# Keys and values loaded and sorted per batch item in a Sinkhorn attention kernel with a maxout layer behind it

## The chip, the cores and the metric

The kernel runs on one NeuronCore of a Trainium2 chip. The metric is the device time of one execution in microseconds (us), where lower is better. The trace also gives a "span", from the first to the last recorded event; in the profiled runs quoted here it is 1.7 to 2.2 us shorter than the time. TensorE runs the matmuls, VectorE ("DVE" in the profile), ScalarE ("ACT") and GpSimd ("POOL") the rest; "SP" only issues transfers. A transfer issued by SP or ACT is an HWDGE transfer, one issued by GpSimd an SWDGE transfer.

## The reference, cut to what matters

```python
# q, k, v: 4 batch items x 8 heads x 768 tokens x 64, fp32; sort_net: 4 x 8 x 8 x 8
P = sort_net
for _ in range(5):                       # Sinkhorn
    P = exp(P - rowmax(P)); P = P / rowsum(P); P = P / colsum(P)
k_sorted = einsum('bhij,bhjcd->bhicd', P, k_blocks)   # 8 blocks of 96 tokens
v_sorted = einsum('bhij,bhjcd->bhicd', P, v_blocks)
attn = softmax(q_block @ k_sorted_block.T / 8)        # block i with block i only
x = (attn @ v_sorted_block).transpose(0, 2, 1, 3).reshape(3072, 512)
out = maximum(x @ w1, x @ w2) @ w_out                 # 512 -> 1024 -> 512
```

The kernel rewrites the last line as relu(x @ (w1 - w2)) @ w_out + x @ (w2 @ w_out), so that one half of the hidden products is computed once for the weights instead of per token.

Of the kernel before, what the change touches and what calls it, by code (L numbers as in the profile page):

```python
# [15 lines left out]
def kernel(  # L16
# [16 lines left out]

# [16 lines left out]
    NSB = 2  # L50
# [5 lines left out]
    big = ctx.enter_context(tc.tile_pool(name="big", bufs=1))  # L56
    qpool = ctx.enter_context(tc.tile_pool(name="qpool", bufs=2))
# [13 lines left out]
    fill = const.tile([128, 512], FP32, tag="fill", name="fill")  # L71
# [33 lines left out]

    def load_q(b):
        t = qpool.tile([128, H, R * D], BF16, tag="q_raw", name="q_raw")
        nc.gpsimd.dma_start(out=t, in_=q[b].rearrange("h (p r) d -> p h (r d)", r=R))
        q_raw[b] = t

    k_raw = big.tile([128, BLK * D], BF16, tag="k_raw", name="k_raw")
    v_raw = big.tile([128, BLK * D], BF16, tag="v_raw", name="v_raw")
    k_src = k.rearrange("b (a par) (j c) d -> par (b a) j (c d)", par=2, j=NB)
    v_src = v.rearrange("b (a par) (j c) d -> par (b a) j (c d)", par=2, j=NB)

    def load_k(sb, chunks):
        n = BLK * D // 3
        for ci in chunks:
            for par in range(2):
                nc.gpsimd.dma_start(  # L120
                    out=k_raw[par * 64 : par * 64 + 64, ci * n : (ci + 1) * n],
                    in_=k_src[par, sb * 8 : sb * 8 + 8, :, ci * n : (ci + 1) * n],
                )

    VCH = 3

    def load_v(sb, chunks):
        n = BLK * D // VCH
        for ci in chunks:
            for par in range(2):  # L130
                nc.gpsimd.dma_start(
                    out=v_raw[par * 64 : par * 64 + 64, ci * n : (ci + 1) * n],
                    in_=v_src[par, sb * 8 : sb * 8 + 8, :, ci * n : (ci + 1) * n],
                )
# [13 lines left out]
    def load_w_columns(dst, src, t):  # L148
# [6 lines left out]
    load_v(0, range(VCH))  # L155
    ident = const.tile([128, 128], BF16, tag="ident", name="ident")
    make_identity(nc, ident)

    mask16 = const.tile([128, 16], BF16, tag="mask16", name="mask16")
    nc.gpsimd.memset(mask16, 1.0)  # L160
    nc.gpsimd.affine_select(
        out=mask16, in_=mask16, compare_op=ALU.is_ge, fill=0.0, base=0,
        pattern=[[-NB, 16]], channel_multiplier=1,
    )
    nc.gpsimd.affine_select(
        out=mask16, in_=mask16, compare_op=ALU.is_ge, fill=0.0, base=NB - 1,
        pattern=[[NB, 16]], channel_multiplier=-1,
    )
    load_q(0)
    load_k(0, range(3))  # L170


    v_dc = big.tile([128, D * BLK + 32], BF16, tag="v_dc", name="v_dc")

    def turn_v(eng, c0, c1):
        dst = v_dc[:, 0 : D * BLK].rearrange("p (d c) -> p d c", c=BLK)[:, :, c0:c1]
        src = v_raw.rearrange("p (c d) -> p d c", d=D)[:, :, c0:c1]
        if eng == "A":
            nc.scalar.copy(out=dst, in_=src)
        else:  # L180
            nc.vector.tensor_copy(out=dst, in_=src)

    for t in range(4):
        load_w_columns(w2_sb, moe_w2, t)
        load_w_columns(w1_sb, moe_w1, t)
    load_w(wo_sb, moe_w_out)
    load_q(1)


# [3 lines left out]
    maskJ = const.tile([128, NB], FP32, tag="maskJ", name="maskJ")  # L193
    sels = []
# [17 lines left out]
    def selections():  # L212

        nc.vector.reduce_sum(
            out=maskJ, in_=ident.rearrange("p (m j) -> p j m", j=NB), axis=AX.X
        )
        for sb in range(NSB):
            sel = const.tile([G, 2, 8, NB], BF16, tag=f"sel{sb}", name=f"sel{sb}")
            src = ident[0:G, sb * 16 : sb * 16 + 16].rearrange("p (gp par) -> p par gp", par=2)
            for par in range(2):  # L220
                nc.vector.tensor_copy(
                    out=sel[:, par], in_=src[:, par, :].to_broadcast([G, 8, NB])
                )
            sels.append(sel)
# [3 lines left out]
    def block_diagonals(sb, n=0):  # L228

        pe = ps_f32("pe")  # L230
        keep_streaming(pe, n)
        nc.tensor.matmul(
            pe[:, 0 : NB * NB],
            sels[sb].rearrange("p a g j -> p (a g j)"),
            p_bf.rearrange("p i j -> p (i j)"),
            start=True,
            stop=True,
        )
        pm = const.tile([128, NB, NB], FP32, tag=f"pm{sb}", name=f"pm{sb}")
        nc.vector.tensor_tensor(  # L240
            out=pm,
            in0=pe[:, 0 : NB * NB].rearrange("p (i j) -> p i j", j=NB),
            in1=maskJ.to_broadcast([128, NB, NB]).transpose([0, 2, 1]),
            op=ALU.mult,
        )
        pt = const.tile([128, NB], FP32, tag=f"pt{sb}", name=f"pt{sb}")
        nc.vector.reduce_sum(out=pt, in_=pm, axis=AX.X)
        bv = const.tile([128, 16, NB], BF16, tag=f"bv{sb}", name=f"bv{sb}")
        nc.vector.tensor_tensor(
            out=bv,  # L250
            in0=mask16.to_broadcast([128, 16, NB]),
            in1=pt.to_broadcast([128, NB, 16]).transpose([0, 2, 1]),
            op=ALU.mult,
        )
        bk = const.tile([128, 8, NB], BF16, tag=f"bk{sb}", name=f"bk{sb}")
        nc.vector.tensor_tensor(out=bk, in0=bv[:, 0:8, :], in1=bv[:, 8:16, :], op=ALU.add)
        bd_v[sb] = bv.rearrange("p m i -> p (m i)")
        bd_k[sb] = bk.rearrange("p m i -> p (m i)")



    kT = big.tile([128, 64 * BLK + 32], BF16, tag="kT", name="kT")
    nc.vector.memset(kT[:, 64 * BLK :], 0.0)
    nc.vector.memset(v_dc[:, D * BLK :], 0.0)
    e_bufs = []
    for n in range(NE):
        t = big.tile([BLK, 8 * BLK + 32], BF16, tag=f"e{n}", name=f"e{n}")
        nc.vector.memset(t[:, 8 * BLK :], 0.0)
        e_bufs.append(t)
    v_sb = big.tile([BLK, 128, D + 2], BF16, tag="v_sb", name="v_sb")  # L270
    nc.vector.memset(v_sb[:, :, D : D + 1], 1.0)
    xT = big.tile([128, B, 2, HP, TCH], BF16, tag="xT", name="xT")

    def q_transposes(b, half):
# [3 lines left out]
        qv = q_raw[b].rearrange("p h (r d) -> p h r d", r=R)  # L278
        ps = ps_bf16("tq_ps")
        for n in range(2 * R):  # L280
            hp, r = half * 2 + n // R, n % R
            for h2 in range(2):
                nc.tensor.matmul(  # L283
                    ps[h2 * 64 : h2 * 64 + 64, n * 128 : (n + 1) * 128],
                    qv[:, 2 * hp + h2, r, :],
                    ident,
                    is_transpose=True,
                    start=True,
                    stop=True,
                )  # L290
# [7 lines left out]
    def sort_k(sb, t, n=0):  # L298
        kv = k_raw.rearrange("p (c d) -> p c d", d=D)
# [3 lines left out]
        for c in range(16):  # L303
            for par in range(2):
# [5 lines left out]
                    bd_k[sb][r0 : r0 + 64, :],  # L310
# [4 lines left out]
            kT[:, 0 : 64 * BLK].rearrange("p (m c) -> p m c", c=BLK)[:, :, t * 16 : (t + 1) * 16],  # L315
            ps.rearrange("p (c m) -> p m c", m=64),
            1024,
        )

    def sort_v(sb, t, n=0):  # L320
        ps = ps_f32("v_ps")
        keep_streaming(ps, n)
        for d in range(8):
            nc.tensor.matmul(  # L324
                ps[:, d * 128 : (d + 1) * 128],
                v_dc[:, (t * 8 + d) * BLK : (t * 8 + d) * BLK + 128],
                bd_v[sb],
                start=True,
                stop=True,
            )  # L330
        evac(
            v_sb[:, :, t * 8 : (t + 1) * 8],
            ps[0:BLK].rearrange("p (d m) -> p m d", m=128),
            1024,
        )
# [3 lines left out]
    def scores(b, u, n=0):  # L339
        ih, hp = divmod(u, HP)  # L340
        gp = (b % 2) * 4 + hp
        ps = ps_f32("s_ps")
        keep_streaming(ps, n)
        for ii in range(4):
            i = ih * 4 + ii
            for h2 in range(2):
                nc.tensor.matmul(  # L347
                    ps[:, h2 * 512 + ii * BLK : h2 * 512 + (ii + 1) * BLK],
                    kT[h2 * 64 : h2 * 64 + 64, (gp * 8 + i) * BLK : (gp * 8 + i) * BLK + 128],
                    qT[b][h2 * 64 : h2 * 64 + 64, hp, :, i * PB : (i + 1) * PB],  # L350
# [13 lines left out]
    def values(b, u, n=0):  # L364
        ih, hp = divmod(u, HP)
        gp = (b % 2) * 4 + hp
        e = e_tiles.pop((b, u))
        ps = ps_f32("o_ps")
        keep_streaming(ps, n)
        for h2 in range(2):  # L370
            for ii in range(4):
# [3 lines left out]
                    v_sb[:, h2 * 64 + gp * 8 + ih * 4 + ii, 0:65],  # L375
# [8 lines left out]
        x = xpool.tile([BLK, 4, 2, D], BF16, tag="x", name="x")  # L384
        nc.vector.tensor_tensor(  # L385
            out=x.rearrange("p i t d -> p t i d"),
            in0=ov[:, :, :, 0:D],
            in1=rs.to_broadcast([BLK, 2, 4, D]),
            op=ALU.mult,
        )  # L390
        load["D"] += 900
        x_tiles[b, u] = x

    def x_transposes(b, t, eng=None):

        ih, hh = divmod(t, 2)
        ps = ps_bf16("tx_ps")
        for n in range(2):
            x = x_tiles.pop((b, t * 2 + n))
            for ii in range(4):  # L400
                m = n * 4 + ii
                nc.tensor.matmul(  # L402
# [249 lines left out]
```

## The kernel before: the parts that the change touches

GpSimd loads everything, casting fp32 to bf16. Keys and values come for two batch items at once. The 64 rows (head group x block) of even heads go to partitions 0 to 63, those of odd heads to 64 to 127.

```python
k_src = k.rearrange("b (a par) (j c) d -> par (b a) j (c d)", par=2, j=NB)
def load_k(sb, chunks):                  # load_v is the same
    n = BLK * D // 3
    for ci in chunks:
        for par in range(2):
            nc.gpsimd.dma_start(
                out=k_raw[par * 64 : par * 64 + 64, ci * n : (ci + 1) * n],
                in_=k_src[par, sb * 8 : sb * 8 + 8, :, ci * n : (ci + 1) * n])
# order of issue: v of items 0 and 1, identity, q of item 0, k of items 0 and 1,
# w2 and w1 by columns, w_out, q of item 1; the rest of q, k, v later
```

The matmuls that sort need "block diagonals" made of P. For v, the tokens are first "turned" (d and c swapped by a strided copy). The program's order fixes what each engine does next:

```python
for it in range(4):
    sinkhorn(it)
    if it == 1: selections()
turn_v("A", 0, 8); sinkhorn(4); turn_v("A", 8, 24); turn_v("D", 24, 32)
block_diagonals(0, 8 * 512)              # 8 x 512 columns of fill ahead of it
... # four more turns, on ACT ("A") and VectorE ("D")
for t in range(8):
    sort_v(0, t, 4 * 512 if t == 0 else 0)
    if t in (3, 5): q_transposes(0, (t - 3) // 2)
for t in range(6):
    sort_k(0, t, {2: 384, 4: 512}.get(t, 0))
... # scores, values and transposes of item 0, then the loop over items:
    # MoE products ("units") of item b, between which stand "steps" of item b + 1
```

`keep_streaming(ps, n)` multiplies a tile of zeros, n columns long, only to keep TensorE busy ("fill"). All matmul results go through four PSUM buffers in turn; to "evict" one is to copy its result to SBUF, by ACT or VectorE. `p_bf` is the finished P in bf16. "MoE" is the code's name for the maxout layer; its "h products" are the hidden ones, and its "weight product" is w2 @ w_out. The "granted clock" is the share of its full clock that TensorE is allowed.

The softmax here doesn't subtract the row's maximum and nothing guards it: scores larger than these inputs give would overflow.

## Time and profile before

| | before |
|---|---|
| time, median of 3 runs | 191.15 us (190.85 to 194.3) |
| span of the profiled run | 189.5 us |
| first MoE product starts | 37.11 us |
| start of the last eviction that waits for TensorE | 185.06 us |
| TensorE, VectorE, ACT busy | 94%, 48%, 46% |

Until 37 us the kernel waits for loads and fills TensorE with zeros; after it TensorE does useful work nearly without a gap.

### The profile page before, as it was taken

The page shows a single profiled execution, that of the slowest core. Times are in us where ns is not written, and L with a number is a line of the kernel's source. Part 1 is how long each engine was busy: PE and PEld are TensorE (multiplying, and loading weights), DVE is VectorE, ACT ScalarE, POOL GpSimd, SP SyncE. Part 2 cuts the span into 40 slices and gives each one's busy share as a digit, 9 for nine tenths or more (in the row PEclk, how much of TensorE's full clock was granted, in tenths as well). Part 3 has the DMA queues.
Part 4 walks back from the last instruction along what each step waited for, and adds up shares of the span by engine and source line. Part 5 has one row for each costly group of instructions (what it writes and reads, how often), then busy time and mean ns, then how long its engine had stood idle before and what let it go on. Part 6 is the DMA issues. An engine that isn't in the chain of part 4 may idle for free.

```text
span 189.5 us, 4458 instructions
## 1 busy us (share of the span) xinstructions
PE 177.5 (94%) x1992; PEld 105.5 (56%) x1992; DVE 90.5 (48%) x172; ACT 88.0 (46%) x103; POOL 25.8 (14%) x47
## 2 busy tenths in 40 slices
PE   6989996799999999999999999999999999999990
PEld 3436755667645455467776445467655456654440
DVE  4887944853431552991476155445553133430030
ACT  3286846877345323059977414237634132631100
POOL 7732465312430000000000000000000000000000
PEclk9999999999999999999999999999999999999998
DMA  2999999999999922230000030230000322000241
GB/s 38 171 200 213 207 197 194 204 205 214 210 209 201 193 58 84 111 112 3 3 3 0 0 114 0 111 114 0 3 0 3 111 111 93 22 0 0 111 156 69
DMA packets 16243, 19.17 MB, mean 101 GB/s; under 512 B 2400, under 2 KB 11616, under 8 KB 16224
## 3 DMA queue, kind: packets, MB, share of 16 engines
q0 software_dynamic: 12896, 12.59, 40.1%
q1 hardware_dynamic: 3328, 6.30, 8.9%
q8 instruction: 15, 0.25, 0.5%
q14 instruction: 4, 0.03, 0.1%
HBM read 25.17 MB, written 6.29 MB: 166 GB/s over the span
## 4 chain that ended last, share of the span: by engine, by line
PE 75%; DMA 11%; DVE 5%; ACT 4%; issue 2%; POOL 1%; ACTq 0%; POOLq 0%
PE out_ps L503 23%; PE h_ps L475 22%; PE out_ps L511 11%; DMA k_raw<-in_k_dram 7%; PE wc_ps L448 4%; DMA v_raw<-in_v_dram 4%; PE o_ps L372 3%; PE s_ps L347 3%; PE tx_ps L402 2%; PE k_ps L307 2%; PE v_ps L324 2%; PE tq_ps L283 2%; DVE o L98 1%; ACT qT L96 1%; PE tw_ps L427 1%
## 5 line engine op out<-in xcount | busy, mean ns | idle before, releaser
L503 PE MATMUL out_ps<-wo_sb,g 128*128 128x512 bf16 x192 | 45.4, 379 | 1.6 <-DVE o L98 0.9
L475 PE MATMUL h_ps<-xT,w_sb 128*128 128x384 bf16 x256 | 45.8, 326 | 0.5 <-ACT xT L96 0.4
L355 ACT ACTIVATE e<-s_ps 96x768 bf16<-96x768 f32 x32 | 24.7, 806 | 23.7 <-PE s_ps L347 23.7
L475 PEld LDWEIGHTS <-w_sb 128*128 128x128 bf16 x256 | 23.7, 98 | 15.1 <-issue 0.4
L503 PEld LDWEIGHTS <-g 128*128 128x128 bf16 x192 | 17.9, 97 | 21.0 <-issue 1.7
L511 PE MATMUL out_ps<-wc,xT 128*128 128x512 bf16 x96 | 24.6, 379 | 0.0
L385 DVE TENSOR_TENSOR x<-o_ps,rs 96x512 bf16<-96x512 f32 x32 | 22.0, 686 | 1.1
L485 ACT ACTIVATE g<-h_ps 128x768 bf16<-128x768 f32 x19 | 15.5, 814 | 15.0 <-PE h_ps L475 14.2
L487 DVE TENSOR_SCALAR g<-h_ps 128x768 bf16<-128x768 f32 x13 | 12.5, 958 | 19.6 <-PE h_ps L475 19.6
L96 ACT COPY o<-out_ps 128x1024 f32<-128x1024 f32 x7 | 7.1, 1013 | 26.8 <-PE out_ps L511 22.3
L383 DVE RECIPROCAL rs<-o_ps 96x8 f32<-96x8 f32 x32 | 6.4, 200 | 23.3 <-PE o_ps L372 23.3
L511 PEld LDWEIGHTS <-xT 128*128 128x128 bf16 x96 | 9.4, 98 | 11.3
L372 PEld LDWEIGHTS <-e 96*128 96x128 bf16 x256 | 11.7, 98 | 3.4
L372 PE MATMUL o_ps<-v_sb,e 96*128 96x65 bf16 x256 | 13.5, 194 | 0.1
L98 DVE COPY o<-out_ps 128x1024 f32<-128x1024 f32 x4 | 4.9, 1225 | 17.2 <-PE out_ps L511 17.2
L96 ACT CAST v_sb<-v_ps 96x1024 bf16<-96x1024 f32 x11 | 10.7, 1022 | 4.0 <-PE v_ps L324 4.0
L347 PE MATMUL s_ps<-qT,kT 64*128 64x96 bf16 x256 | 10.0, 205 | 1.6 <-issue 1.2
L78 PE MATMUL pe<-fill 128*128 128x512 f32 x16 | 9.9, 785 | 1.5 <-DVE fill L72 1.5
L98 DVE COPY xT<-tx_ps 128x768 bf16<-128x768 bf16 x7 | 6.7, 955 | 7.7 <-PE tx_ps L402 7.7
L347 PEld LDWEIGHTS <-kT 64*128 64x128 bf16 x256 | 6.2, 94 | 7.1 <-issue 4.6
L98 DVE CAST kT<-k_ps 128x1024 bf16<-128x1024 f32 x5 | 6.1, 1225 | 8.0 <-PE k_ps L307 7.9
L96 ACT COPY xT<-tx_ps 128x768 bf16<-128x768 bf16 x9 | 7.2, 795 | 4.2 <-PE tx_ps L402 4.2
(70 smaller groups left out, 174.5 us busy)
## 6 DMA issues: line engine op xcount, KB each, us to landing
out_dram<-o SPq DMA_DIRECT2D x11, 512.0 KB, 2.8
v_raw<-in_v_dram POOLq DMA_DIRECT2D x12, 256.0 KB, 11.6
q_raw<-in_q_dram POOLq DMA_DIRECT2D x4, 768.0 KB, 13.9
k_raw<-in_k_dram POOLq DMA_DIRECT2D x12, 256.0 KB, 12.0
w_sb<-in_moe_w_dram POOLq DMA_DIRECT2D x8, 256.0 KB, 10.6
wo_sb<-in_moe_w_out_dram POOLq DMA_DIRECT2D x2, 512.0 KB, 12.4
out_dram<-o SPq DMA_DIRECT2D x2, 256.0 KB, 2.0
p_sb<-in_sort_net_dram SPq DMA_DIRECT2D x1, 8.0 KB, 1.7
```

Of the source, the lines that this page charges most:

```text
L78: nc.tensor.matmul(ps[:, 0:w], fill[:, 0:128], fill[:, 0:w], start=True, stop=True)
L96: nc.scalar.copy(out=out_ap, in_=in_ap)
L98: nc.vector.tensor_copy(out=out_ap, in_=in_ap)
L347: nc.tensor.matmul(ps[:, h2 * 512 + ii * BLK : h2 * 512 + (ii + 1) * BLK], kT[h2 * 64 : h2 * 64 + 64, (gp * 8 + i) * BLK : (gp * 8 + i) * ...
L355: nc.scalar.activation(out=e[:, 0 : 8 * BLK].rearrange("p (t f) -> p t f", t=2), in_=ps[0:BLK].rearrange("p (t f) -> p t f", t=2)[:, :, 0 ...
L372: nc.tensor.matmul(ps[:, h2 * 512 + ii * 65 : h2 * 512 + (ii + 1) * 65], e[:, (h2 * 4 + ii) * BLK : (h2 * 4 + ii) * BLK + 128], v_sb[:, h2 ...
L385: nc.vector.tensor_tensor(out=x.rearrange("p i t d -> p t i d"), in0=ov[:, :, :, 0:D], in1=rs.to_broadcast([BLK, 2, 4, D]), op=ALU.mult,)
L475: nc.tensor.matmul(ps[:, m * 512 : m * 512 + TCH], w1_sb[:, hp, fb * 128 : (fb + 1) * 128], xT[:, b, ch, hp, :], start=(hp == 0), stop=(hp ...
L485: nc.scalar.activation(out=g, in_=src, func=AF.Relu)
L487: nc.vector.tensor_scalar(out=g, in0=src, scalar1=0.0, scalar2=None, op0=ALU.max)
L503: nc.tensor.matmul(dst, g_tiles[b, ch, fb // 2][:, fb % 2, off : off + 128], wo_sb[:, fb, :], start=(fb == 0), stop=False,)
L511: nc.tensor.matmul(dst, xT[:, b, ch, hp, off : off + 128], wc[:, hp, :], start=False, stop=(hp == HP - 1),)
```

## The change

The intent: load and sort only what batch item 0 needs before the first MoE product, and put the sorting of item 1 between the products. Keys lie as 128 rows (head, block, half of the block's tokens). SP loads the first pieces of v and half of q of item 0 as fp32 (HWDGE) beside GpSimd's loads. Output units are cut in halves so that steps stand more evenly between them. The tile of zeros for the fill becomes bf16 instead of fp32: the first fill was 16 matmuls of 512 columns in 9.85 us, and is now 24. Cut to its core:

```diff
+    for m in range(HB // VF):                       # 3 pieces of 16 tokens
+        t = opool.tile([128, 2, 512], FP32, tag="o", name="v_f32")
+        nc.sync.dma_start(out=t[0:64, :], in_=v_src[0, :, m * VF * D : (m + 1) * VF * D])
+    for n in range(2):
+        nc.sync.dma_start(
+            out=q_f32[:, n * 4 : n * 4 + 4, :], in_=q_half[0, :, n * 4 : n * 4 + 4, :])
-    load_v(0, range(VCH))
+    load_v(0, HB)                                   # only tokens 48 to 96 of each block
+    make_identity(nc, ident32)                      # fp32
-    load_q(0)
-    load_k(0, range(3))
+    load_k(0)                                       # item 0 only
+    load_w_columns(w2_sb, moe_w2, 0)
+    load_w_columns(w1_sb, moe_w1, 0)
+    nc.gpsimd.dma_start(out=q_bf, in_=q_half[1])    # other half of q, bf16
     ... # other weights
+    load_v(1)
+    load_k(1)
     load_q(1)
 ...
+    def q_first(t, n=0):                            # fp32 products with the identity
+        keep_streaming(ps, n)
+        ...
+                nc.tensor.matmul(ps[...], q_f32[:, hp + 4 * h2, r * D : (r + 1) * D],
+                                 ident32, start=True, stop=True)
 ...
+        if it == 0:
+            masks(0)
+            q_out.append(q_first(0, 12288))         # 24 x 512 columns of bf16 fill
+        if it == 1:
+            q_out.append(q_first(1))
+            turn_v(first, "A", 0, 8, v_f32[0])      # ACT, between the Sinkhorn exps
 ...
+        4: [lambda: block_diagonals(1), lambda: turn(second, 0)],
+        5: [lambda: turn(second, 24), lambda: selections(2)],
+        6: [lambda: turn(second, 48), lambda: pair_q(1, 0), lambda: pair_q(1, 1)],
+        7: [lambda: turn(second, 72), lambda: block_diagonals(2), lambda: selections(3)],
+        8: [lambda: block_diagonals(3), lambda: load_v(2), lambda: load_v(3)],
 ...
+    def moe_out_last(ti, pieces):                   # last two tiles, in pieces
+                o = opool.tile([128, w], FP32, tag=f"o{n0}{m}", name="o", bufs=1)
```

## The prediction

> **What bounds the kernel now.** I read the engine totals first, then the slices, then the chain of waits in order of time, and last the timeline of single engines in the first 40 us.
>
> ```profile
> PE 177.5 (94%) x1992; PEld 105.5 (56%) x1992; DVE 90.5 (48%) x172; ACT 88.0 (46%) x103; POOL 25.8 (14%) x47
> PE   6989996799999999999999999999999999999990
> DMA  2999999999999922230000030230000322000241
> ```
>
> TensorE looks full from end to end, but its first eight slices (4.74 us each) hold many matmuls of the zero tile "fill", which only keep it running. The transfers are dense just there. The chain says what those slices wait for:
>
> ```profile
> 1.32 1.29 POOL v_raw L131 x2
> 2.62 7.11 DMA v_raw<-in_v_dram
> 9.73 0.28 issue
> 10.01 13.94 DMA k_raw<-in_k_dram
> 23.95 0.04 issue
> 24.00 1.27 PE k_ps L307 x63
> ...
> 36.26 0.81 ACT xT L96
> 37.07 0.04 issue
> 37.11 1.46 PE h_ps L475 x8
> ```
>
> Two transfers, 7.1 and 13.9 us, hold the path until 24.0 us; then come the key sort, evictions, attention of batch item 0, and at 37.11 us the first useful MoE product. From there the chain is nearly all TensorE. Its timeline from 37.11 us to the last eviction's start (185.06 us, row below) is 147.95 us, and the idle entries of its rows add up to 2.1 us. So there are three parts: a head of 37.1 us bound by loads, a body of 148 us bound by TensorE, and a drain of 4.4 us (185.06 to 189.5).
>
> ```profile
> 185.06 0.37 ACT L520 COPY o<-out_ps 128x256 f32<-128x256 f32 x1 [2.22 <-PE out_ps L511]
> 185.47 0.42 DVE L521 COPY o<-out_ps 128x256 f32<-128x256 f32 x1 [2.17 <-ACT o L520]
> ```
>
> **What the Trainium skill says.** "DMA: Bandwidth & Descriptors" (section "SWDGE vs HWDGE vs iDMA") says that only GpSimd can issue a transfer that casts; hence the HWDGE loads must land as fp32 tiles, as the diff has them. Its section "Issuing engines are not separate DMA queues" says that all transfers share the same 16 engines, so a second issuing queue saves issue time, not bandwidth. I therefore count bytes over both queues. No run yet shows the mix. "SBUF — State Buffer" (section "Door 1: The DMA port swizzle") says 64 partitions reach half of the ports; v now lands on 64 partitions, but with a cast only half of the read bytes are written, so I expect little loss except in the three fp32 pieces. "ScalarE: Activation LUTs" (section "What ACT_TABLE_LOAD costs") gives 186 ns + 0.833 ns per element; the trace agrees for PSUM sources (128x1024 in 1013 ns), but not for the turning of v from SBUF (128x1024 in 1952 ns, 128x512 in 1060: about 1.74 ns per element).
>
> **The head, step by step.** Keys or values of one batch item are 8x768x64x4 B = 1.57 MB. Before, 3.15 MB of v, 1.57 of q and 3.15 of k (7.9 MB) precede the last key sort. After, v of item 0, half of q and k of item 0 do: 3.9 MB. The chain gives 3.15 MB in 7.11 us = 0.44 MB/us, so I estimate 3.9/0.44 = 9 us, that is, k landed near 12 us instead of 24 us. That takes the loads off the path, for the following is later.
>
> The Sinkhorn chain: exp at 2.53 us, 1.76 us per iteration when nothing is between (2.53, 4.29, 6.05 in the trace), p_bf at 11.9 us before. The new masks add eight small VectorE operations of about 0.2 us each in three places; each place hides 0.3 us in the wait for exp, as the 1.1 us inserted before cost 0.6. So p_bf stays at 11.9 to 12.3 us. Block diagonals: 0.25 us for the matmuls, then five VectorE operations (0.21, 0.21, 0.22, 0.22, 0.22 plus gaps) give 13.7 us; before it was 13.4 us.
>
> ACT then turns v columns 24 to 32 (1.06 us), evicts q (0.8), turns 32 to 48 and 48 to 64 (up to 1.95 each), evicts q again (0.8): done at 16.0 to 17.4 us, by whether fp32 sources run at 0.83 or 1.74 ns per element. VectorE turns 32 columns (about 2.0 us), free at 15.7 us. Then seven sort evictions (1.0 ACT, 1.23 VectorE), exp of four scores (0.81 each on ACT) and the q_second eviction (1.45) run on two engines. Walking engine by engine and with four PSUM buffers: last v eviction at 21.2 to 22.8 us, first values at 22 to 23.6, four normalisations at 0.9 us each to 25.9 to 27.5, two transposes and their evictions (0.8 each) to 27.4 to 29.0. The second pair of those is waited for only inside the first MoE product, and 0.43 us of fill precede it. First MoE product at 27.0 to 28.6 us; I take 27.8, a gain of 9.3 us on 37.1.
>
> **What is not gained but moved into the body.** Spacings on TensorE's timeline per matmul: k sort 19.5 ns, v sort 54.4, scores 32.2, values 37.5, q transposes 30.4, w2 transposes 56. For the new 64-column v sort I take 33 ns (values with 65 columns are that without their group's start).
> Keys of item 1: 96 x 19.5 = +1.87 us. Values of item 1: 64 x 33 = +2.11. Scores 5 to 7 and values 4 now follow the first product: 24 x 32.2 + 8 x 37.5 = +1.07. One w2 transpose group goes into the head: 16 x 56 = -0.90. Paired q transposes of three items: 24 x 55 instead of 48 x 30.4, -0.42. Three more block-diagonal matmuls of 0.13: +0.39. Values of items 2 and 3: 128 x 33 - 64 x 54.4 = +0.74. Sum +4.9 us. The MoE products themselves (42.1, 62 and 7.0 us for h, out and the weight product) stay.
>
> VectorE gets six copies of q (0.9 us each by the program's own estimate) and four half-filled turns (1.5 us) more; at 48% and 46% the two eviction engines have room. Half units move steps more finely, which can remove some of the 2.1 us idle, while new turns and q copies may add some: I leave 2.2.
>
> **Drain.** The last tile's two evictions ran one after the other (0.41 + 0.42). They now read 128 columns each into own tiles and issue from two queues: 0.6 us less, 3.8 instead of 4.4.
>
> **Sum.** 27.8 + (147.95 - 2.1) + 4.9 + 2.2 + 3.8 = 184.5 us of span. The timed run of the same profile was 191.2 against 189.5: +1.7. That makes 186.2, and I name 186.0.
>
> **Rivals.** First, *the removed loads were hidden anyway*: TensorE is 94% busy. Against it: about 17 us of that busy time are fill matmuls (9.9 + 3.7 us and smaller rows), and the chain names two DMAs. It would leave 190 to 191. Second, *the wait moves to ACT and VectorE in the head*, which I believe in part: evictions and turning become the bound from 13 to 27 us. If ACT also waits for the fp32 pieces between Sinkhorn exps, or VectorE's turn of 32 columns delays the first eviction, the product starts near 31 us and the time is 189. Third, *the second round of loads is late*: q of item 1 is last in the initial queue, 15.7 MB in all, at 0.41 MB/us (205 GB/s written, read double) 38 us plus 2.6, near 41 us, just when its pairing copy stands on VectorE, after seven products. A late arrival blocks VectorE and then PSUM: +1 to 2 us, 187 to 188. Fourth, in the other direction: *the author's fill counts fit a shorter wait than mine* (256 columns, 0.11 us, before each sort), so the head may end at 25 to 26 us: 184.
>
> **Range and chances.** The body's sum is good to about 1.5 us, the head to about 2, the new idle to 1. I take 182.8 to 189.2 as the range. Faster by over 2% means below 187.3; my sum lies only 1.3 below it, hence 0.66. Slower by 2% would need a head longer than before: 0.03.
>
> **What would show it.** Right: k landed by about 13 us and no long DMA piece in the chain after it; VectorE and ACT pieces between 13 and 27 us; first h product at 27 to 29 us; out products' count and spacing as before; TensorE idle in the body 2 to 3 us; drain below 4. Wrong: the first h product after 31 us, or a body (first h product to last eviction) above 155 us, or waits of VectorE on q_raw near 41 us.

## The result, and the profile after

The changed kernel takes 202.71 us (median of 4 runs, 201.18 to 202.86) where the kernel before takes 191.0 us (4 runs, 190.82 to 194.3; the 194.3 is 1.8% above the fastest and counts as slow). The ratio of the fast runs is 1.0598, with a 95% interval of 1.0534 to 1.0663. A ratio here is the mean time of one kernel's fast runs over that of the other's fast runs of the same rounds, so it is not quite the ratio of the quoted medians. The change is 6% slower; I had expected it to be 2.7% faster.

The page of the changed kernel, engine totals and two rows of the 40 slices (5.02 us each):

```profile
PE 179.5 (89%) x2072; PEld 107.6 (54%) x2093; DVE 94.5 (47%) x189; ACT 94.9 (47%) x114; POOL 25.5 (13%) x40
...
PE   7806969899959989999999999999999999999991
...
PEclk9985996999996999999999999999999999999999
```

The third slice of TensorE is empty; its granted clock is 0.5 in the fourth, and low again in slices 7 and 13 (0.6). Before, there was no such hole. The chain of waits in order of time says why (start, length, what):

```profile
3.03 0.63 SPq L167
3.67 0.04 issue
3.71 13.69 DMA q_f<-in_q_dram
17.40 0.04 issue
17.45 4.43 PE tq_ps L336 x46
21.88 0.26 issue
22.13 0.23 PE pe L292 x2
```

This answers to the two DMA pieces of the kernel before, which ended at 23.95 us. The second of the two loads that bring the first half of q (0.4 MB of fp32 each) holds the path until 17.4 us, and the transposes until 21.9 us. The keys were not the wait: GpSimd's row shows their three pieces landing by about 11.0, 12.6 and 14.3 us, the last here (it ends GpSimd's wait before the next issue):

```profile
14.28 0.74 POOL L186 DMA_DIRECT2D w_sb<-in_moe_w_dram  x1 [0.92 <-DMA k_raw<-in_k_dram]
```

The matmul of the block diagonals, which the keys need, stands behind the transposes of q in TensorE's order, though its input was ready at 12.74 us. TensorE's own timeline (start, length, line, operation, tile, form, count, wait before):

```profile
1.19 8.25 PE L78 MATMUL tq_ps<-fill 128*128 128x512 bf16 x24 [1.19 <-DVE fill L72]
14.82 0.66 PE L336 MATMUL tq_ps<-ident,q_f 128*64 128x128 f32 x2 [5.37 <-DMA q_f<-in_q_dram]
17.45 4.43 PE L336 MATMUL tq_ps<-ident,q_f 128*64 128x128 f32 x46 [1.97 <-DMA q_f<-in_q_dram]
39.11 1.75 PE L616 MATMUL h_ps<-xT,w_sb 128*128 128x384 bf16 x8
```

The fill ends at 9.4 us, TensorE waits, and the first MoE product starts at 39.11 us, where I had 27.8. The table of stretches gives busy times, then the granted clock, the DMA share and GB/s:

```profile
18.00:20.00 2.00, 2.00 (x22) 2.00 (x20) 0.00 (x0) 0.00 (x0) 0.74 (x1) 0.50 1.59 193
...
32.00:34.00 2.00, 2.00 (x43) 1.86 (x42) 1.59 (x2) 1.93 (x3) 0.54 (x1) 0.50 1.23 230
...
62.00:64.00 2.00, 2.00 (x10) 0.90 (x8) 0.96 (x1) 0.96 (x1) 1.43 (x3) 0.50 1.31 202
```

The clock is a half while the fp32 transposes run, and also after two later waits (of 1.4 us before 29.9 us, and of 2.3 us before 60.5 us).

The second loss is in the body. VectorE's timeline from the fifth product unit on:

```profile
50.27 0.96 DVE L632 TENSOR_SCALAR g<-h_ps 128x768 bf16<-128x768 f32 x1 [2.94 <-PE h_ps L616]
...
51.91 2.90 DVE L217 COPY v_dc<-v_raw 64x1536 bf16<-64x1536 bf16 x2
...
55.21 1.49 DVE L217 COPY v_dc<-v_raw 64x1536 bf16<-64x1536 bf16 x1
56.71 1.03 DVE L377 COPY q_pair<-q_raw 128x1536 bf16<-128x1536 bf16 x2
57.77 1.45 DVE L217 COPY v_dc<-v_raw 64x1536 bf16<-64x1536 bf16 x1
59.25 0.36 DVE L302 TENSOR_TENSOR pm<-pe,maskJ 128x64 f32<-128x64 f32 x2
...
60.24 0.21 DVE L277 COPY sel_k<-ident 32x128 bf16<-32x128 bf16 x1
```

VectorE works without a pause from 50.3 to 60.4 us, and the last of these, a selection for batch item 3, is what TensorE waits for:

```profile
60.51 0.20 PE L292 MATMUL pe<-p_bf,sel_k 32*128 32x64 bf16 x1 [2.29 <-DVE sel_k L277]
```

The keys of item 3 are sorted only from 137 us on. The wait is there only because of where the program puts the matmul. After it the clock is a half, and the eight matmuls of the second weight product take 3.3 us instead of 1.8.

Third, the end:

```profile
194.44 3.91 SPq L682 DMA_DIRECT2D out_dram<-o  x2
...
196.57 0.37 ACT L679 COPY o<-out_ps 128x256 f32<-128x256 f32 x1 [9.61 <-DMA out_dram<-o]
```

ACT evicts the first half of the last tile only when the store of the tile before has landed. Both ask for a tile with the tag "o00", of which there is one.

The sum of the differences from my own sum: first product +11.3 us (39.1 for 27.8). From there to the time at which TensorE is done (196.3 us; the last four matmuls start at 195.70, and an undisturbed eviction starts 0.63 us after that start) it is 157.2 us, where I had 145.85 + 4.9 + 2.2 = 152.95: +4.3 us. From there to the end 4.4 for 3.8: +0.6 us. Together +16.2 us, which is 200.7 less 184.5.

### The profile page after: what moved, and what is told of

It reads as the page before. It is cut to its first block, busy times and chain, and to the rows that moved or that the text cites. A ratio compares the mean times of both kernels' runs of the same rounds, so it can differ in the third digit from the quotient of the medians.

```text
span 200.7 us, 4674 instructions
## 1 busy us (share of the span) xinstructions
PE 179.5 (89%) x2072; PEld 107.6 (54%) x2093; DVE 94.5 (47%) x189; ACT 94.9 (47%) x114; POOL 25.5 (13%) x40
## 3 DMA queue, kind: packets, MB, share of 16 engines
q1 hardware_dynamic: 4624, 7.68, 11.3%
## 4 chain that ended last, share of the span: by engine, by line
PE 73%; DVE 9%; DMA 8%; issue 4%; ACT 3%; SPq 1%; ACTq 0%; DVEq 0%
PE out_ps L643 28%; PE h_ps L616 18%; DMA q_f<-in_q_dram 7%; PE v_ps L435 5%; PE wc_ps L584 3%; PE s_ps L463 3%; DVE v_dc L217 3%; PE o_ps L488 3%; PE k_ps L414 3%; PE tq_ps L390 2%; PE tx_ps L534 2%; PE tq_ps L336 2%; DVE x L514 1%; ACT o L96 1%; DMA out_dram<-o 1%
## 5 line engine op out<-in xcount | busy, mean ns | idle before, releaser
L643 PE MATMUL out_ps<-wo_sb,g 128*128 128x512 bf16 (+1 forms) x185 | 46.2, 370 | 1.8 <-ACT o L96 0.7
L630 ACT ACTIVATE g<-h_ps 128x768 bf16<-128x768 f32 x28 | 22.7, 812 | 22.2 <-PE h_ps L616 22.2
L471 ACT ACTIVATE e<-s_ps 96x768 bf16<-96x768 f32 x32 | 24.2, 804 | 17.5 <-PE s_ps L463 17.4
L643 PE MATMUL out_ps<-wc,xT 128*128 128x512 bf16 (+1 forms) x100 | 24.8, 370 | 0.0
L98 DVE CAST v_sb<-v_ps 96x1024 bf16<-96x1024 f32 x8 | 9.7, 1218 | 18.9 <-PE v_ps L435 18.9
L96 ACT COPY o<-out_ps 128x1024 f32<-128x1024 f32 x6 | 6.1, 1012 | 22.8 <-issue 13.3
L217 DVE COPY v_dc<-v_raw 64x1536 bf16<-64x1536 bf16 (+2 forms) x9 | 13.6, 1537 | 0.1
L336 PE MATMUL tq_ps<-ident,q_f 128*64 128x128 f32 x48 | 5.1, 375 | 7.3 <-DMA q_f<-in_q_dram 7.3
L129 POOL DMA_DIRECT2D q_raw<-in_q_dram x3 | 4.2, 1387 | 56.8 <-DVE q_pair L377 54.6
L96 ACT CAST v_sb<-v_ps 96x1024 bf16<-96x1024 f32 x8 | 8.1, 1013 | 6.4 <-PE v_ps L435 6.4
L435 PEld LDWEIGHTS <-v_dc 64*128 64x128 bf16 x256 | 8.5, 97 | 4.1 <-issue 3.9
L96 ACT CAST kT<-k_ps 128x1024 bf16<-128x1024 f32 x10 | 10.0, 1012 | 0.5 <-PE k_ps L414 0.5
## 6 DMA issues: line engine op xcount, KB each, us to landing
v_raw<-in_v_dram POOLq DMA_DIRECT2D x6, 384.0 KB, 11.9
q_f<-in_q_dram SPq DMA_DIRECT2D x2, 384.0 KB, 12.7
```

The lines of the kernel that those rows point to most:

```text
L96: nc.scalar.copy(out=out_ap, in_=in_ap)
L98: nc.vector.tensor_copy(out=out_ap, in_=in_ap)
L217: nc.vector.tensor_copy(out=dst, in_=src)
L336: nc.tensor.matmul(ps[h2 * 64 : h2 * 64 + 64, m * 128 : (m + 1) * 128], q_f32[:, hp + 4 * h2, r * D : (r + 1) * D], ident32, start=True, s ...
L435: nc.tensor.matmul(ps[:, m * 64 : (m + 1) * 64], v_dc[r0 : r0 + 64, d * BLK : d * BLK + 128], bd_v[b][r0 : r0 + 64, :], start=True, stop=True,
L471: nc.scalar.activation(out=e[:, 0 : 8 * BLK].rearrange("p (t f) -> p t f", t=2), in_=ps[0:BLK].rearrange("p (t f) -> p t f", t=2)[:, :, 0 ...
```

## The experiments

Twelve runs of eleven kernels, all edits of the changed one. Times are medians of all executions of each run; only e11 (two) and e12 (one) had slow ones, and their medians over fast ones alone are 186.1 and 187.2 us. The kernel before gave 190.8 to 194.8 us beside them (its fast executions 190.8 to 193.3, and once 996 us beside e12), and the record's verdict on each of these runs against it, where it gives one, is "unclear". That spread and the changed kernel's own (1.7 us) mean that time differences under about 1 us are not separated, and I rely on the trace for those. e12 ran on another chip than the rest. All passed the test of the result, e1 in spite of itself (see there).

| run | what differs from the change | time, us | q turned from | first product |
|---|---|---|---|---|
| the change | | 202.71 | 17.45 | 39.11 |
| e1 | q in runs of 3072 B | 199.09 | 15.25 | 35.51 |
| e2 | weights wait for q | 201.03 | 16.09 | 37.70 |
| e8 | q ahead of v on SP's queue | 195.51 | 7.87 | 32.59 |
| e9 | GpSimd loads nothing before q | 195.8 (one run, state unknown) | 9.88 | 34.11 |
| e3 | q by GpSimd, bf16 | 190.44 | 10.28 | 27.88 |
| e4 | fill until q lands | 198.67 | 17.67 | 35.52 |
| e5 | masks of items 2 and 3 later | 200.22 | 17.69 | 39.83 |
| e6 | own output tiles | 202.14 | 17.78 | 39.27 |
| e7 | e3 + e5 + e6 | 186.29 | 9.69 | 27.24 |
| e10 | e7, and v by GpSimd too | 187.56 | 9.03 | 29.41 |
| e12 | e10, identity first | 187.41 | 10.40 | 27.34 |

"q turned from" is the start of the (second group of the) first transposes.

### Why does q land so late?

**e1_long_rows.** The first question was whether the short runs of q (768 B) get a small share of the engines.

```diff
-            out=q_f32[:, n * 4 : n * 4 + 4, :], in_=q_half[0, :, n * 4 : n * 4 + 4, :]
+            out=q_f32.rearrange("p h x -> p (h x)")[:, n * 768 : n * 768 + 768],
+            in_=q[0, 0:4].rearrange("h (a x) d -> (h a) (x d)", a=32)[:, n * 768 : n * 768 + 768],
```

> Same bytes of q on the HWDGE queue, but in runs of 3072 B per partition instead of 768 B (the result is wrong on purpose). Theory T1 (the 16 engines take turns between the GpSimd queue and the HWDGE queue, so short runs get a small share): both q tiles land by 9 to 11 us instead of 14.8 and 17.4, and the time falls by 6 to 8 us to about 195. Rival T2 (all bytes queued at the same time share the bandwidth, run length does not matter): q still lands at 15 to 17 us and the time stays within 1 us of 202.7.

The transposes start at 13.04 and 15.25 us instead of 14.82 and 17.45, and the time is 199.09 us. (In its profile, the fastest of its four executions, the clock also stays at 1.00 after the wait in the body, see e5; that part of the gain is not due to q.) So run length has a part of some 2 us in q's arrival, and neither theory is right as put. (The result was accepted although q's tokens were mislaid on purpose: the scores are so small that the softmax hardly sees them, which is my reading and was not tested. It is a warning not to take "correct" as proof for q's path.)

**e2_queue_waits.**

```diff
     load_k(0)
+    seen = const.tile([128, H], FP32, tag="seen", name="seen")
+    nc.gpsimd.tensor_copy(out=seen, in_=q_f32[:, :, 0])
     load_w_columns(w2_sb, moe_w2, 0)
```

> Runs of 768 B as in the change, but GpSimd issues the weight loads only after q has landed (a small copy that reads q stands ahead of them). T1 and T2 both: q lands earlier, at 9 to 11 us, since only the second half of v and k compete; the first MoE product moves from 39.1 us to 31 to 33 us unless the weights, which start later, become the wait. Rival T3 (short runs are slow by themselves, whoever competes): q still lands near 17 us and the time rises.

A miss: q lands only 1.4 us earlier (transposes from 16.09 us) and the first product comes at 37.7 us. The weights are not what q mainly competes with. What is left in front of it or beside it are v's pieces on its own queue, and the second half of v and the keys on GpSimd's.

**e8_q_first** and **e9_alone** separate these two.

```diff
+    for n in range(2):                              # e8: q's two loads ahead of v's three
+        nc.sync.dma_start(out=q_f32[...], in_=q_half[...])
     for m in range(HB // VF):
         ...
```

> The change, but on the HWDGE queue the two q loads stand ahead of the three pieces of v. Theory T4 (q is late mostly because it is queued behind v on its own queue): q lands by 8 to 10 us and v's last piece by 13 to 15 us; ACT then waits for v between the exps of the Sinkhorn chain, p_bf comes at 14 to 17 us instead of 12.7, and the time is 196 to 199. Rival (the share against the GpSimd queue alone): q still lands after 12 us.

```diff
-    load_v(0, HB)                                   # e9
     make_identity(nc, ident32)
+    nc.gpsimd.tensor_copy(out=seen, in_=q_f32[:, :, 0])
+    load_v(0, HB)
```

> The disputed cost by itself: GpSimd issues none of its loads until q has landed, so v's pieces and q have the engines alone. If the competition of the GpSimd queue is the cause, all 1.6 MB land by 6 to 8 us. If the HWDGE loads are slow by themselves (short runs, 64 partitions), q lands after 10 us. The time of the whole kernel is worse in either case (v's second half and k start late), 200 to 210 us.

With q first (e8) it lands 3.6 and 5.5 us after its issue at 1.19 and 1.65 us, before the fill is over. The wait then sits on v, as ACT's timeline shows, and the block diagonals move with it:

```profile
4.13 0.26 ACT L225 ACTIVATE p_sb<-p_sb 32x64 f32<-32x64 f32 x1 [0.82 <-DVE p_sb L233]
9.60 1.10 ACT L215 CAST v_dc<-v_f 64x512 bf16<-64x512 f32 x1 [5.22 <-DMA v_f<-in_v_dram]
```

p_bf comes at 15.8 us instead of 12.7, since ACT must turn v before the next exp. That is theory T4, with its price. It is still 7 us faster than the change, because q's turn no longer ends at 21.9 us.

With nothing from GpSimd beside it (e9), q's transposes run from 9.88 us:

```profile
9.88 2.83 PE L338 MATMUL tq_ps<-ident,q_f 128*64 128x128 f32 x46 [0.52 <-DMA q_f<-in_q_dram]
```

So of the 17.4 us, 7.6 come from GpSimd's loads beside it (17.45 less 9.88). Since holding back the weights alone gave 1.4 (e2), the larger part is due to v's second half and the keys. This and the place in the queue are not two parts of a sum: with q first it landed at about 7 us although GpSimd's loads ran beside it (e8). But even alone, v's and q's 1.57 MB in fp32 (v 0.79, q 0.79) took until 9.9 us from an issue at 1.19: an estimate of 0.18 MB/us from this trace. The pages count the bytes as they land: 211 GB/s in e9's second slice (4.9 to 9.7 us), and 171 to 213 in slices 2 to 8 of the kernel before, where each landed byte stands for two that were read. Per landed byte the two are about equal; per value, fp32 took about twice as long. (The rate is no fixed one: in e8's second slice, with both kinds under way, it was 265.) I had expected 6 to 8 us. Its time, 195.8 us in the one run, was better than I expected.

**e3_q_cast** takes q off that queue.

```diff
-        nc.sync.dma_start(out=q_f32[:, n * 4 : n * 4 + 4, :], in_=...)   # two of them
+    nc.gpsimd.dma_start(out=q_f32, in_=q_half[0])    # q_f32 now bf16, ahead of v and k
 ...
-                    ident32, start=True,
+                    ident, is_transpose=True, start=True,
```

> The first half of q comes by GpSimd's queue with a cast to bf16, ahead of v and k, and is turned by bf16 transposes. My theory (the HWDGE load of q in fp32 holds the head): q lands by 5 to 6 us, its transposes end before p_bf at 12.7 us, the first MoE product starts at 28 to 31 us and the time is 191 to 194. Rival (the head is bound by the Sinkhorn chain, turning and evictions anyway, q only covers it): first product after 34 us, time above 197.

```profile
10.28 0.86 PE L334 MATMUL tq_ps<-ident,q_f 128*64 128x128 bf16 x24 [0.89 <-DMA q_f<-in_q_dram]
...
27.88 1.75 PE L615 MATMUL h_ps<-xT,w_sb 128*128 128x384 bf16 x8
```

q lands at 10.2 us, later than the 5 to 6 us I expected, but ahead of p_bf, and 24 bf16 transposes take 0.9 us. The first product comes at 27.88 us. The time, 190.44 us, is 12 us below the change's; the ratio to the kernel before is 0.993 (0.981 to 1.005), so this alone gives the loss back and no more. The edit changes three things at once: the queue, q's place at the front, and the type, in which q lands as half the bytes and is transposed faster. Which of them gives how much is not shown; q in fp32 at the front of GpSimd's queue was not run.

### What the clock costs

**e4_fill_on.**

```diff
-            q_out.append(q_first(0, 12288))
+            q_out.append(q_first(0, 33280))
```

> The fill ahead of the first q transposes goes on until q arrives (65 instead of 24 matmuls of 512 columns, to about 18 us). Theory (after 7 us of waiting the array runs at half its clock): the 46 fp32 transposes take 2.2 us instead of 4.4, the clock between 20 and 40 us is 1.0 instead of 0.96 and 0.83, first product 2 to 4 us earlier, time 199 to 200.5. Rival (the transposes are slow because they are fp32): still 4.4 us, and the time within 1 us of 202.7.

```profile
17.67 2.93 PE L336 MATMUL tq_ps<-ident,q_f 128*64 128x128 f32 x48
```

With q landing as late as in the change, 48 fp32 transposes take 2.93 us instead of 4.43 for 46, the granted clock is 1.00 in every stretch from 0 to 40 us, the first product comes at 35.5 us and the time at 198.67 us: 4.0 us are the price of letting TensorE go idle while it waits. (2.93 is above the 2.2 that I expected: fp32 transposes are slow too, 61 ns each against 36 in bf16.) "TensorE: Matmul & The Clock Gate" (section "Part 1: The HAM clock gate") of the Trainium skill says that the array runs at half its clock after an idle window and at full clock after a busy one, each of about 3.4 us; the 0.50 and 1.00 of these traces agree with the two levels.

### The body

**e5_later_masks.**

```diff
-        7: [lambda: turn(second, 72), lambda: block_diagonals(2), lambda: selections(3)],
-        8: [lambda: block_diagonals(3), lambda: load_v(2), lambda: load_v(3)],
+        7: [lambda: turn(second, 72)],
+        8: [lambda: load_v(2), lambda: load_v(3)],
+        13: [lambda: block_diagonals(2), lambda: selections(3)],
+        16: [lambda: block_diagonals(3)],
```

> The change as it is, but the block diagonals of items 2 and 3, with their selection, stand five and eight units later in the program. Theory (between the seventh product unit and the first weight product VectorE has 10 us of turns, q copies and mask work in one row, and TensorE waits in order for the last of it): the 2.3 us wait before the matmul of the block diagonals at 60.5 us goes, the cold weight product after it (3.1 us for 8) goes back to 1.8, and the time falls by 3 to 4 us to about 199. Rival (TensorE only waits for the next thing on VectorE, the q transposes or their eviction): less than 1 us.

```profile
58.62 1.50 PE L390 MATMUL tq_ps<-ident,q_pair 128*128 128x128 bf16 x24
59.96 1.89 PE L584 MATMUL wc_ps<-wo_sb,w2T 128*128 128x512 bf16 x8
```

No wait stands before the q transposes, and the weight product after them is back at 1.8 us for eight (59.96 to 61.78, where the next row starts). The idle entries of TensorE's rows in the body fall from 4.8 to 2.5 us. The time falls by 2.5 us to 200.22, less than the 3 to 4 expected. In the profile the stretch from the first product to the end of the span is 3.9 us shorter (157.7 for 161.6), as expected, but the fp32 transposes happened to take 5.03 us and the first product came 0.7 us later than in the change's profile.

The wait itself is sure, the half clock after it is not. Eight profiles have the same wait of 2.3 us (the change, e1 to e4, e6, e8, e9); the eight matmuls of the weight product after it took 3.3 to 3.5 us in four of them (the change, e2, e6, e8), 2.4 in e4, and 1.9 in e1, e3 and e9.

### The end

**e6_own_tiles.**

```diff
-                o = opool.tile([128, w], FP32, tag=f"o{n0}{m}", name="o", bufs=1)
+                o = opool.tile([128, w], FP32, tag=f"o{ti}{n0}{m}", name="o", bufs=1)
```

> The change with one edit: each piece of the last two output tiles has an SBUF tile of its own, where before two of them shared one by name. Theory (the eviction of the last tile's first half waits 0.8 us for the store of the tile before): that wait goes from the trace, the span ends within 3.8 us of TensorE's end instead of 4.6, and the time is 0.6 to 1.0 us below the change's 202.7. Rival (the last store is the bound and starts no earlier): no difference.

```profile
195.21 0.37 ACT L679 COPY o<-out_ps 128x256 f32<-128x256 f32 x1 [8.07 <-PE out_ps L643]
```

The eviction now waits for TensorE and not for a store, and the span ends 3.3 us after TensorE (199.8 less 196.51) where it was 4.4. The time is 202.14 us against 202.71: in the expected direction, but within the spread of the runs.

### Together

**e7_three** has the edits of e3, e5 and e6, and **e11_three_again** is the same file once more.

> Three edits together: q's first half by GpSimd with a cast and bf16 transposes, the block diagonals of items 2 and 3 later, and an own tile for each piece of the last two output tiles. If the three losses are separate they add up: 190.4 (measured for the cast alone) minus 2.5 to 4 minus 0.8 gives 185.5 to 187, faster than the kernel before by 2 to 3%. If the waits only hand over to each other: 189 to 190.

> The three edits once more, with more rounds and beside the two others on one chip: 186.3 within 0.7 us, and 2 to 3.5% faster than the kernel before.

186.29 us (four runs, 186.0 to 186.68), a ratio of 0.973 (0.965 to 0.981) to the kernel before; again 186.4 us (seven runs, 185.63 to 189.36, two of them slow, the profiled one among these) and 0.972 (0.964 to 0.979). The three gains, 12.3, 2.5 and 0.6 us one by one, would give 187.4; so they add up, and this version is faster than both kernels. How far it is past 2% over the kernel before is not settled ("unclear" by the record): against the steadiest runs of the kernel before (190.8 to 191.2 us, granted clock above 0.99) it is 2.4 to 2.5%. Its marks in TensorE's and ACT's timelines:

```profile
27.24 1.75 PE L615 MATMUL h_ps<-xT,w_sb 128*128 128x384 bf16 x8
...
180.53 0.27 ACT L678 COPY o<-out_ps 128x128 f32<-128x128 f32 x1 [0.94 <-PE out_ps L642]
```

First product at 27.2 us (my 27.8), 153.3 us from there to the last eviction that TensorE releases (my 152.95), and 3.5 us to the end of the span at 184.0 (my 3.8). That 186.3 meets my 186.0 so closely is in part luck: the span is 0.5 us below mine, and the time is 2.0 us above the span where I took 1.7; and it is not the kernel that I predicted. It is also not safe from the clock: in the slow, profiled run of e11, q's transposes start only at 11.76 us, 3.8 us after the fill, and the clock is 0.50 from 12 to 16 us. Why q was late there is not known.

### Does any HWDGE load of fp32 help?

**e10_all_cast** loads v's first pieces by GpSimd with a cast too, and **e12_ident_first** also builds the identity ahead of the issues.

```diff
-        t = opool.tile([128, 2, 512], FP32, tag="o", name="v_f32")
-        nc.sync.dma_start(out=t[0:64, :],
+        t = big.tile([128, 1024], BF16, tag=f"v_first{m}", name="v_f32")
+        nc.gpsimd.dma_start(out=t[0:64, :],
```

> The three edits, and the three first pieces of v also by GpSimd's queue with a cast, behind q: no first load by HWDGE is left but the sort network. If the fp32 pieces on HWDGE win anything, it is that v comes beside q: without them v's pieces land at 8 to 11 us, ACT waits in the Sinkhorn chain and the time is 1 to 3 us above the three edits' 186.3. If fp32 landing only takes engine time away from q and k: within 0.7 us, or faster.

```diff
+    make_identity(nc, ident32)                      # e12: ahead of every load
     q_raw, qT = {}, {}
 ...
-    make_identity(nc, ident32)
```

> All first loads of v, q and k by GpSimd with casts, as in the run before it, but the identity is built ahead of the load issues. In that run the identity stood behind five issues, and its copy on ACT (5.49 us) held the second exp by 1.6 us, which I take to be the whole of its 1.2 us loss. Theory: the exp comes at 4.1 us, p_bf at 11.3 to 11.6 us, and the time is 185.3 to 186.8, level with the three edits' 186.4; then the HWDGE pieces of v win nothing. Rival: the loss is from v or q landing later, and the time stays above 187.

The edit puts v's three pieces ahead of q on GpSimd's queue, not behind it as I wrote. In e10 they landed 3.3 to 3.9 us after their issue, where the HWDGE ones took 5.3 to 7.7 in the change and 4.4 to 8.4 in e7; and q's transposes ran from 9.03 us, no later than in e7 (9.69). But the identity came late behind five issues, so the second exp started at 5.70 us instead of 4.04, TensorE waited 2.6 us for p_bf, its clock was 0.50 from 12 to 16 us, and the first product came at 29.4 us: 187.56 us. So the late exp, which I took for the whole loss, was not all of it. e12 mends that: first product at 27.34 us, level with e7. Its time is nevertheless 187.41 us (186.13 to 188.99), against the expectation. Its trace names another wait:

```profile
48.17 1.51 PE L388 MATMUL tq_ps<-ident,q_pair 128*128 128x128 bf16 x24 [1.60 <-DVE q_pair L375]
...
47.08 1.03 DVE L375 COPY q_pair<-q_raw 128x1536 bf16<-128x1536 bf16 x2 [2.16 <-DMA q_raw<-in_q_dram]
```

q of item 1, the last load of the first round, is 2 us late, and TensorE waits 1.6 us for the copy. In e7 the same copy stands at 44.83 us and waits for nothing. So whether the HWDGE pieces of v win something is not settled: in the head they do not (27.34 for 27.24 us). The longer queue of GpSimd's loads alone does not explain the later wait: e10, with the same loads in the same queue, issued this one at 28.54 us and had it 16.0 us later, at 44.5 us, where e12 issued it at 30.07 and had it at 47.1. Why e12 was later stays open.

## Why the prediction was wrong, point by point

**The step that failed** is in "The head, step by step": "I estimate 3.9/0.44 = 9 us, that is, k landed near 12 us instead of 24 us. That takes the loads off the path". I put all bytes of both queues into one sum at the rate of casting loads and then followed only k. The load that mattered was q. It stood last on its queue, in fp32, behind v's fp32 pieces and beside GpSimd's loads, and landed at 17.4 us. Alone it would have been 9.9 us (e9), and first in its queue about 7 us (e8). From the rule that all queues share the same engines I drew the total, but not the order in which each transfer completes. The keys themselves were not far off: they landed at about 14.3 us for my 12.

The rate in that sum was misread too. The 7.11 us of the chain is the landing of one piece of v, not of the six that make 3.15 MB; in GpSimd's row, waits for four of the pieces end between 10.0 and 14.0 us, the last here:

```profile
13.98 0.81 POOL L151 DMA_DIRECT2D w_sb<-in_moe_w_dram  x1 [0.89 <-DMA v_raw<-in_v_dram]
```

The page's 171 to 213 GB/s of landed bytes are 0.34 to 0.43 MB/us of values read with a cast, not 0.44. And bytes had to be counted as they land: v's and q's fp32 loads are 1.57 MB, the cast half of v and k 1.18, together 2.75 MB where 3.9/2 is 1.97. An estimate from the changed kernel's page (95 GB/s in the first slice of 5.02 us, some 220 after it) puts 2.75 MB at about 15 us; by 17.4 us 3.2 MB had landed, weights among them.

**The second miss in the same step** is that I let TensorE's fill stand for granted. It was cut for an earlier arrival: it ended at 9.4 us, TensorE cooled, and the transposes of q, which I took as done before p_bf, took 4.4 us and held back everything behind them in TensorE's order. With fill the same late q costs 4.0 us less (e4). Together the two put the first product 11.3 us later. The rest of that step was right within its ranges or 0.1 us beside them, as e3 (first product at 27.88 us) and e7 (27.24) show once q is out of the way. In e7 p_bf came at 11.8 us (my 11.9 to 12.3), ACT was done with its turns at 16.5 (16.0 to 17.4), the last eviction of sorted v ended at 22.0 (21.2 to 22.8) and the normalisations at 26.3 (25.9 to 27.5). What landing on 64 partitions costs, which I had named, no run tests by itself.

**The body.** As a total, the sum of the moved work held: 153.3 us measured in e7 for 152.95. What failed was "at 48% and 46% the two eviction engines have room". As an average that stays true (47% and 47% after), but VectorE had a solid row from 50.3 to 60.4 us, and TensorE's order made it wait for the row's last member. The wait (2.29 us), the half clock after it (some 1.5 us in the weight product) and small changes elsewhere make the 4.3 us; e5 takes out the wait, and with it the half clock, which does not follow in every profile.

**The drain.** I expected 0.6 us less and did not see that two pieces share a tile by their tag. It cost what it was to save (4.4 us as before); with own tiles it is 3.3 to 3.5 us.

**The rivals.** The first (the loads were hidden anyway) is refuted by e3 and e7, whose heads are 9.2 and 9.9 us shorter than before (the fill rows of the kernel before add up to 18.6 us, not about 17). The second named "if ACT also waits for the fp32 pieces between Sinkhorn exps": it did, for 2.2 us, and p_bf came at 12.7 us, but that was covered by q. The third (q of item 1 late near 41 us) did not happen in the changed kernel, since its head was late itself; in e12 it is a real wait. The fourth took the fill counts as a sign that the author's waits were shorter than mine. In these runs they were longer, and the fill was too short by 8 us. None of the four had the first load of q in it, and so the whole range was missed.

**What I had said would show it wrong** did: a first product after 31 us and a body above 155 us.

## What to carry to other kernels

When loads are put on two queues, follow each transfer on its own: what is ahead of it in its queue, what runs beside it, in which type it lands, and which engine's program order stops when it is late. Count a transfer's bytes as they land: here v and q in fp32 took about as long per landed byte as casting loads, and so about twice as long per value. Taking q off the second queue, with a cast and to the front, gained 12 us, and leaving v there won nothing in the head. A fill that keeps TensorE warm is tuned to an arrival time; when a load moves, the fill must move too. And in an in-order program, work that is not needed for a long time must not stand ahead of work that is, even when every engine is half idle.

## What the Trainium skill lacked or had wrong

- "DMA: Bandwidth & Descriptors" (section "Issuing engine by pattern") says that HWDGE is generally faster. Here v's fp32 pieces of 256 KB landed 5.3 to 7.7 us after their issue by HWDGE, and 3.3 to 3.9 us by GpSimd with a cast to bf16 (e10). As the cast halves the landed bytes and other loads ran beside them, this does not show the sentence wrong. No page gives the price of landing in fp32 against casting: 211 GB/s landed in fp32 (e9, second slice), and 171 to 213 with a cast, which reads twice that (the kernel before, slices 2 to 8).
- "ScalarE: Activation LUTs" (section "What ACT_TABLE_LOAD costs") gives 0.833 ns per element; no page gives a figure for ACT with a strided source in SBUF. ACT's turn of v took 1.95 us for 1024 elements from fp32 and 2.01 us from bf16 alike, about twice that rate. My guess that fp32 sources might run at the full rate was wrong.
- "TensorE: Matmul & The Clock Gate" (section "Part 1: The HAM clock gate") speaks of an idle window of about 3.4 us before the clock falls. Here shorter waits sufficed: one of 1.4 us was followed by a granted clock of 0.50 (the change, 31 to 34 us), and one of 2.3 us by 0.50 in the change (62 to 64 us) but by 1.00 in e3. Whether that is the window's free running, which the page describes, is not tested. The page gives no spacing for fp32 transposes: 61 ns warm (2.93 us for 48) and 96 ns in the change (4.43 for 46).
